# Attention and MoE on one core: the kv and z products a slot later, the numerator two slots behind the projection, and stage-one transfers in written order

## The chip, the cores and the metric

The program runs on one core of one Trainium2 chip. The metric is device time of one execution in microseconds (us), measured over the whole program. A profiled execution also gives a span, from the first to the last instruction of the program, and a trace of every engine: PE (matmul), PEld (its weight loads), DVE (VectorE), ACT (ScalarE), POOL (GpSimd), SP (the engine whose queue issues nearly all transfers here), and the DMA engines.

## What is computed

A linear attention over 8 batches of 8 heads, 576 positions, head size 64, whose output is the input of a two-layer MoE block of 4608 tokens. Cut to what matters:

```python
def phi(x):
    proj = np.einsum('bhsd,df->bhsf', x, w_phi)               # 64 -> 128 features
    proj = proj - np.max(np.abs(proj), axis=-1, keepdims=True)
    return np.concatenate([np.exp(proj), np.exp(-proj)], axis=-1)
q_p, k_p = phi(q), phi(k)
kv  = np.einsum('bhsf,bhsd->bhfd', k_p, v)
z   = np.sum(k_p, axis=2)
num = np.einsum('bhsf,bhfd->bhsd', q_p, kv)
den = np.einsum('bhsf,bhf->bhs', q_p, z)[..., None] + 1e-06
x   = (num / den)                                              # to [4608, 512]
h   = x @ w_in                                                 # [4608, 2048]
g   = np.maximum(h, 0.0) + alpha * np.minimum(h, 0.0)
out = g @ w_out                                                # [4608, 512]
```

## The kernel before

The work has two stages. **Stage one** runs over 32 pairs of heads (`i`, four pairs for each batch of the attention). Beside the pairs it runs the first 5 of 16 slices of the MoE's middle dimension for the first seven blocks of 512 tokens (`ffn1_units(c)`, c from 0 to 6), and it decodes weights. **Stage two** runs the other slices for all tokens, after a short piece that finishes the first five slices for the last two blocks.

The order of stage one is written by hand. Each piece of work has a time in *slots*, where pair i has its projections from slot i on. `AT` gives the times of a pair's pieces relative to i. All pieces of all pairs are sorted by time (`todo`) and recorded in that order. For PE this order is kept as it is (`manual_schedule`, line 449). The other engines, the SP queue among them, get an order from a scheduler that plans with estimated durations; a few instructions (`keep_in_program_order`) stand in the written place on their engine too. Each engine and the SP queue then work strictly in their order: one that waits holds up all that stands behind it.

The pieces of pair i, with their lines:

- `load` (192, 194): the transfers of raw keys and queries (`raw`, two buffers) and of `v` (three buffers).
- `project`, five times (207, 215, 216): PE multiplies into `pj` (two PSUM buffers), DVE takes the largest absolute value `m` and subtracts it, giving `t`. The first chunks hold keys, the last two queries, the third both.
- `k_exp` (232, 227): ACT makes `xk` (one buffer) and `k`. `k_sum` (240 to 242): the sums y and z, on POOL for i under 7, on DVE after that.
- `k_acc` (250) and `k_z` (260): PE multiplies into `kv`. `kv_out` (266) copies it to `ks`; `kv_turn` (271, 273) transposes it, giving `sf`.
- `q_exp` (287, 281, 289, 283): PE turns the queries, ACT makes `qf`.
- `num` (297, 304): the numerator, copied to `s`. `den` (311, 319, 321): the denominator; ACT copies it to `ds`, and a small transfer moves 9 values for each partition into `d9`.
- `invert` (327 to 332): DVE makes `r9` from `d9`; one transfer stores it to memory (`rec_d`), two read it back spread over partitions (`rr`).
- `finish` (338, 339): POOL multiplies `s` by `rr`, and a transfer stores the result (`x_d`).

A *filler* is one step of the MoE's first slices: three matmuls of 512 columns (367 to 369, or 373 to 375). `STEPS` places ten of them in each slot, so each block of tokens fills four slots (40 steps). A block begins with `fetch`, the transfer of four pairs' results (`xr`, 383), and `split` (389 to 392), in which DVE rounds `xr` to `xh` (line 94) and POOL takes the rest `xl` (line 97), four pieces each. `FL`, `FX` and `FO` place fetch, split and the first filler. I call the slot in which a block is fetched and split a *batch slot*.

`decode` (117 to 141) turns 64-bit weights into two 32-bit halves: a transfer (`raww`, two buffers), one ACT, four DVE and one POOL instruction, then one ACT and one POOL instruction (`w`, or `ow`). 20 blocks of it feed the first five slices, 20 more are stored back to memory (`w_d`, 141) for stage two.

## Time and profile before

| what | value |
|---|---|
| time, median of three runs | 1311.33 us (1309.7 to 1312.77) |
| time of the profiled execution | 1311.5 us |
| its span | 1309.7 us |
| PE busy | 1206.5 us (92%) |
| DVE, ACT, POOL busy | 658.2, 505.6, 345.1 us |
| mean granted TensorE clock, of full speed | 0.966 |

The profiled execution lies 0.2 us from the median, and 1.8 us of its time lie outside the span. Stage one runs to about 693 us of the span. The granted clock is 1.00 nearly throughout stage two, and lower in parts of stage one.

### The profile page before, as it was taken

Reading aid. Unit: us, or ns where it says so; the run is one execution under the profiler, and the core shown is the slowest. Engines: PE = TensorE matmul, PEld = TensorE weight load, DVE = VectorE, ACT = ScalarE, POOL = GpSimd, SP = SyncE. Lnnn points to the kernel's source line nnn. Section 1 sums busy time; section 2 is a strip of 40 time slices with the busy share of each in tenths; the row PEclk is TensorE's granted clock in tenths of the full one; section 3 lists DMA queues with packets and bytes.
Section 4 is the critical chain, followed back from the end, with each engine's and each line's share of the span. In section 5 each row is a group of like instructions: output and inputs, shape, how many; then the busy total and the mean of one; then the engine's idle time right before and its main releaser. Section 6 shows DMA issues by size and latency. Waiting matters only on the chain.

```text
span 1309.7 us, 16685 instructions
## 1 busy us (share of the span) xinstructions
PE 1206.5 (92%) x6272; PEld 919.4 (70%) x6272; DVE 658.2 (50%) x1112; ACT 505.6 (39%) x1014; POOL 345.1 (26%) x374
## 2 busy tenths in 40 slices
PE   5767799999989999997987999999999999999998
PEld 3434566677767667665755778888888888888886
DVE  4663566657666666667824357323333332323232
ACT  2543363555545455463633344222222222222221
POOL 4563422313132321324513246111111111111110
PEclk7789899999989999998998999999999999999999
DMA  4332334334343533525345032202022020202010
GB/s 154 95 113 85 106 100 154 124 122 126 124 137 109 165 104 102 164 92 174 103 143 191 33 131 63 97 1 97 25 72 71 26 97 1 97 1 97 1 66 32
DMA packets 67808, 124.20 MB, mean 95 GB/s; under 512 B 14224, under 2 KB 19472, under 8 KB 67088
## 3 DMA queue, kind: packets, MB, share of 16 engines
q1 hardware_dynamic: 67008, 117.90, 27.7%
q0 software_dynamic: 720, 5.24, 1.1%
q8 instruction: 49, 0.80, 0.3%
q14 instruction: 31, 0.25, 0.1%
HBM read 89.27 MB, written 33.70 MB: 94 GB/s over the span
## 4 chain that ended last, share of the span: by engine, by line
PE 71%; DMA 10%; DVE 7%; POOL 5%; issue 3%; ACT 2%; SPq 1%; DVEq 0%; POOLq 0%; ACTq 0%
PE h L367 9%; PE h L369 9%; PE h L368 9%; PE po L373 7%; PE po L374 7%; PE po L375 7%; PE pj L207 7%; PE kv L250 3%; DMA rr<-rec_d 3%; PE n L297 3%; PE d L311 2%; DMA xr<-x_d 2%; DMA rec_d<-r 2%; PE o L373 2%; PE o L374 2%
## 5 line engine op out<-in xcount | busy, mean ns | idle before, releaser
L207 PE MATMUL pj<-w_sb,raw 128*128 128x256 f32 x576 | 169.2, 418 | 44.1 <-DVE t L216 21.7
L150 ACT ACTIVATE r<-h 128x512 f32<-128x512 f32 x144 | 86.0, 598 | 283.6 <-PE h L369 283.1
L156 POOL TENSOR_SCALAR r<-r,al 128x512 f32<-128x512 f32 x99 | 73.1, 738 | 433.8 <-ACT r L150 429.0
L157 DVE SCALAR_TENSOR_TENSOR g<-h,r 128x512 f32<-128x512 f32 x99 | 68.2, 689 | 235.7 <-POOL r L156 235.7
L207 PEld LDWEIGHTS pj<-w_sb,raw 128*128 128x128 f32 x576 | 113.3, 206 | 86.6 <-issue 56.7
L215 DVE TENSOR_REDUCE m<-pj 128x4 f32<-128x512 f32 (+1 forms) x160 | 101.1, 635 | 111.3 <-PE pj L207 107.8
L373 PE MATMUL po<-gh,w 128*128 128x512 f32 x396 | 155.6, 393 | 0.0
L374 PE MATMUL po<-gh,w 128*128 128x512 f32 x396 | 155.2, 392 | 0.0
L93 ACT CAST gh<-g 128x512 fp32r<-128x512 f32 x144 | 89.3, 621 | 167.8 <-DVE g L157 134.6
L375 PE MATMUL po<-gl,w 128*128 128x512 f32 x396 | 153.6, 392 | 0.0
L97 DVE TENSOR_TENSOR gl<-g,gh 128x512 fp32r<-128x512 f32 x144 | 102.6, 713 | 72.6 <-ACT gh L93 72.6
L216 DVE TENSOR_TENSOR t<-pj,m 128x512 f32<-128x512 f32 (+1 forms) x160 | 101.2, 633 | 2.8
L367 PE MATMUL h<-x2hl,w 128*128 128x512 f32 x220 | 87.0, 396 | 11.9 <-ACT x2hl L93 11.9
L338 POOL TENSOR_TENSOR s<-s,rr 128x576 f32<-128x576 f32 x31 | 46.4, 1497 | 194.0 <-DMA rr<-rec_d 163.9
L373 PE MATMUL o<-gh,w 128*128 128x512 f32 x180 | 86.0, 478 | 2.1 <-ACT gh L93 1.1
L367 PE MATMUL h<-xh,w 128*128 128x512 f32 x180 | 86.4, 480 | 1.2 <-ACT g L152 1.2
L369 PE MATMUL h<-x2hl,w 128*128 128x512 f32 x220 | 86.7, 394 | 0.0
L368 PE MATMUL h<-x2hl,w 128*128 128x512 f32 x220 | 86.6, 394 | 0.0
L375 PEld LDWEIGHTS po<-gl,w 128*128 128x128 f32 x396 | 74.4, 188 | 17.0
L374 PEld LDWEIGHTS po<-gh,w 128*128 128x128 f32 x396 | 74.4, 188 | 16.8
L373 PEld LDWEIGHTS po<-gh,w 128*128 128x128 f32 x396 | 74.3, 188 | 16.7
L250 PE MATMUL kv<-xk,v 128*64 128x256 f32 x512 | 68.9, 416 | 17.7 <-ACT xk L232 17.7
(82 smaller groups left out, 2228.7 us busy)
## 6 DMA issues: line engine op xcount, KB each, us to landing
raw<-kq_dram SPq DMA_DIRECT2D x32, 576.0 KB
xr<-x_d SPq DMA_DIRECT2D x17, 1024.0 KB
v<-v_dram SPq DMA_DIRECT2D x32, 320.0 KB
rr<-rec_d SPq DMA_DIRECT2D x64, 144.0 KB
x_d<-s SPq DMA_DIRECT2D x32, 288.0 KB
part_d<-os SPq DMA_DIRECT2D x36, 256.0 KB
pt<-part_d SPq DMA_DIRECT2D x9, 1024.0 KB
raww<-w_in_dram SPq DMA_DIRECT2D x32, 256.0 KB
```

What stands on the lines that cost most here:

```text
L93: return act.copy(dst, src)
L97: return eng.tensor_tensor(dst, src, f(hi), op=ALU.subtract)
L207: pe.matmul(ps[:, j].rearrange("p h f -> p (h f)"), lhsT=c["raw"][:, tp * P : (tp + 1) * P], rhs=w_sb, start=True, stop=True,)
L215: dve.tensor_reduce(m, ps, axis=AX.X, op=ALU.max, apply_absolute_value=True)
L216: dve.tensor_tensor(c["t", ch][:, :, j0 : j0 + w].rearrange("p h j f -> p j h f"), ps, m.unsqueeze(3).broadcast_to([P, w, 2, FD]), op=ALU. ...
L250: pe.matmul(c["kv"][h * D : (h + 1) * D, 0], lhsT=c["v"][:, tp, h, :], rhs=c["x", ch][:, :, h, j, :], start=tp == 0, stop=False,)
L367: pe.matmul(ps, lhsT=wt[0][:, ws], rhs=xh, start=n == 0, stop=False)
L368: pe.matmul(ps, lhsT=wt[1][:, ws], rhs=xh, start=False, stop=False)
L369: pe.matmul(ps, lhsT=wt[0][:, ws], rhs=xl, start=False, stop=n == NK - 1)
L373: pe.matmul(ps, lhsT=wt[2][:, ws], rhs=gh, start=first, stop=False)
L374: pe.matmul(ps, lhsT=wt[3][:, ws], rhs=gh, start=False, stop=False)
L375: pe.matmul(ps, lhsT=wt[2][:, ws], rhs=gl, start=False, stop=last)
```

## The change

A pair's pieces are spread over more slots. The products `kv` and `kz` go from 0.48 and 0.50 to 1.17 and 1.18, one slot behind the pair's projections; numerator and denominator go from 1.49 and 1.505 to 2.16 and 2.155, two slots behind. The turned queries (`q`), the turned kv (`kr`), `invert` (`dv`) and `finish` (`x`) follow. `load` moves from 1.3 to 0.95 slots ahead. A block of tokens begins three steps later (`FO`), and its fetch and split stand after the slot's start instead of before it (`FL`, `FX`). `decode` is split: the transfer of the raw weights is an entry of its own, half a slot ahead (`WL`). The SP queue joins PE: in stage one its transfers are issued in written order.

```diff
-WS = 1.4
-W2A = 7.0
+WS = 1.6
+WL = 0.5
+W2A = 8.5
...
-    ld=-1.3,
-    p=(0.0, 0.12, 0.24, 0.80, 0.90),
-    ke=(0.14, 0.25),
-    ks=0.29,
-    q=(1.27, 1.33, 1.39),
-    ka=0.48,
-    n=1.49,
-    kz=0.50,
-    d=1.505,
-    kt=0.51,
-    kr=1.17,
-    dv=1.95,
-    x=2.35,
+    ld=-0.95,
+    p=(0.0, 0.08, 0.50, 0.82, 0.92),
+    ke=(0.20, 0.51),
+    ks=0.515,
+    n=2.16,
+    d=2.155,
+    ka=1.17,
+    kz=1.18,
+    kt=1.185,
+    q=(1.55, 1.62, 1.66),
+    kr=1.75,
+    dv=2.60,
+    x=3.00,
 )
-STEPS = (0.05, 0.08, 0.16, 0.20, 0.30, 0.36, 0.42, 0.45, 0.85, 0.95)
+STEPS = (0.03, 0.06, 0.11, 0.13, 0.52, 0.57, 0.64, 0.70, 0.86, 0.96)
 EARLY = 7
-FO = 4
+FO = 7
 F0 = 3.0
-FL = 0.4
-FX = 0.2
+FL = -0.2
+FX = -0.4
...
+    wraw = {}
+
+    def decode_load(ff, z, o, n):
...
-        ld_ = nc.sync.dma_start(raw.rearrange("p a b -> p (a b)"), (w_in, w_out)[z][ff][:, cs].bitcast(U32))
-        if NF1 <= ff < NF1 + NA:
-            tc.keep_in_program_order(ld_)
+        nc.sync.dma_start(raw.rearrange("p a b -> p (a b)"), (w_in, w_out)[z][ff][:, cs].bitcast(U32))
+        wraw[ff, z, o] = raw
+
+    def decode(ff, z, o, n):
+        tag = f"w{ff}_{z}_{o}"
+        if (ff, z, o) not in wraw:
+            decode_load(ff, z, o, n)
+        raw = wraw.pop((ff, z, o))
+        cs = slice(o, o + n)
...
-                todo.append(((ff + z / 2) * WS, lambda ff=ff, z=z, o=o: decode(ff, z, o, WN)))
+                t = (ff + z / 2 + o / 1024) * WS
+                todo.append((t - WL, lambda ff=ff, z=z, o=o: decode_load(ff, z, o, WN)))
+                todo.append((t, lambda ff=ff, z=z, o=o: decode(ff, z, o, WN)))
...
+        todo.append((t - WL, lambda blk=blk: decode_load(*blk, WN)))
         todo.append((t, lambda blk=blk: decode(*blk, WN)))
...
-    with tc.manual_schedule(engines={mybir.EngineType.PE}):
+    with tc.manual_schedule(engines={mybir.EngineType.PE, mybir.EngineType.SP}):
```

Three places show what moves. The first is PE in the early slots, where no fillers run yet. In the names the digit behind the first letters is the pair: kv3 is the kv product of pair 3, d2 the denominator of pair 2. Before, from the turned queries of pair 2 to its denominator:

```order
L287 MATMUL qt2_1_602<-ident_67,t2_3_514 128x128 x4
L281 MATMUL qt2_t_611<-ident_67,t2_2_434 128x128 x2
L250 MATMUL kv3_616<-xk3_571,v3_365 64x256 x8
L250 MATMUL kv3_616<-k4_1_121,v3_365 64x256 x2
L297 MATMUL n2_0_628<-qf2_589,sf2_579 64x288 x4
L297 MATMUL n2_1_634<-qf2_589,sf2_579 64x288 x4
L260 MATMUL kv3_616<-z3_598,ones_117 64x256 x2
L311 MATMUL d2_666<-qf2_589,sf2_579 32x288 x8
L207 MATMUL pj3_3_686<-w_sb_115,raw3_363 128x256 x2
```

Now, the same products of pairs 2 and 3, which stand behind two projections of pair 4:

```order
L216 MATMUL pj4_0_634<-w_sb_115,raw4_491 128x256 x2
L216 MATMUL pj4_1_654<-w_sb_115,raw4_491 128x256 x2
L320 MATMUL d2_660<-qf2_572,sf2_614 32x288 x8
L306 MATMUL n2_0_674<-qf2_572,sf2_614 64x288 x4
L306 MATMUL n2_1_680<-qf2_572,sf2_614 64x288 x4
L259 MATMUL kv3_686<-xk3_544,v3_346 64x256 x8
L259 MATMUL kv3_686<-k4_1_121,v3_346 64x256 x2
L269 MATMUL kv3_686<-z3_568,ones_117 64x256 x2
L216 MATMUL pj4_2_717<-w_sb_115,raw4_491 128x256
L296 MATMUL qt3_0_730<-ident_67,t3_3_616 128x128 x4
```

The kv product of pair 3 stood in the slot of that pair's own projections; it now stands in pair 4's, and d2 stands ahead of z3 instead of behind it.

The second place is the SP queue around the fetch of the first block of tokens (xr1_0). Before, from the denominator of pair 2:

```order
L321 DMA d9_2_677<-ds2_675 128x1x9
L192 DMA raw5_681<-kq_dram 128x1152
L329 DMA rec_d_58<-r9_2_698 128x9
L332 DMA rr2_702<-rec_d_58 64x576 x2
L339 DMA x_d_57<-s2_627 128x576
L194 DMA v7_1003<-v_dram 128x640
L321 DMA d9_3_824<-ds3_822 128x1x9
L192 DMA raw6_828<-kq_dram 128x1152
L329 DMA rec_d_58<-r9_3_869 128x9
L332 DMA rr3_873<-rec_d_58 64x576 x2
L339 DMA x_d_57<-s3_798 128x576
L383 DMA xr1_0_975<-x_d_57 128x4x512
```

Now, from the denominator of pair 3:

```order
L330 DMA d9_3_820<-ds3_818 128x1x9
L124 DMA raww3_1_256_869<-w_out_dram 128x512
L338 DMA rec_d_58<-r9_3_886 128x9
L341 DMA rr3_890<-rec_d_58 64x576 x2
L124 DMA raww4_0_0_929<-w_in_dram 128x512
L348 DMA x_d_57<-s3_822 128x576
L201 DMA raw7_956<-kq_dram 128x1152
L203 DMA v7_958<-v_dram 128x640
L330 DMA d9_4_977<-ds4_975 128x1x9
L392 DMA xr1_0_1010<-x_d_57 128x4x512
L124 DMA raww4_0_256_1012<-w_in_dram 128x512
L338 DMA rec_d_58<-r9_4_1055 128x9
```

The raw keys of a pair stood behind the denominator's transfer three pairs earlier and now stand behind the store of x_d four pairs earlier; raw weights stand between; the fetch has the next pair's denominator transfer ahead of it.

The third place is DVE around the split of the fourth block of tokens (xh1_3; m17_3 is the m of pair 17, chunk 3). Before:

```order
L215 TENSOR_REDUCE m17_3_3219<-pj17_3_3216 128x4
L216 TENSOR_TENSOR t17_3_3215<-pj17_3_3216,m17_3_3219 128x2x2x128
L94 CAST xh1_3_3222<-xr1_3_3209 128x512 x4
L215 TENSOR_REDUCE m17_4_3255<-pj17_4_3252 128x4
L215 TENSOR_REDUCE m18_0_3273<-pj18_0_3270 128x4
L216 TENSOR_TENSOR t17_3_3215<-pj17_4_3252,m17_4_3255 128x2x2x128
L327 TENSOR_SCALAR d9_16_3205<-d9_16_3205 128x9
L216 TENSOR_TENSOR t18_0_3269<-pj18_0_3270,m18_0_3273 128x2x2x128
```

Now:

```order
L137 TENSOR_SCALAR aw7_0_256_3310<-aw7_0_256_3310 128x256
L138 SCALAR_TENSOR_TENSOR aw7_0_256_3310<-raww7_0_256_3208,aw7_0_256_3310 128x256
L139 TENSOR_SCALAR ew7_0_256_3311<-aw7_0_256_3310 128x256
L140 SCALAR_TENSOR_TENSOR ew7_0_256_3311<-raww7_0_256_3208,ew7_0_256_3311 128x256
L95 CAST xh1_3_3259<-xr1_3_3257 128x512 x4
L224 TENSOR_REDUCE m18_2_3272<-pj18_2_3270 128x2
L249 TENSOR_TENSOR y18_3277<-xk18_3254 128x1024
L225 TENSOR_TENSOR t18_2_3269<-pj18_2_3270,m18_2_3272 128x256
L250 TENSOR_TENSOR z18_3278<-y18_3277 128x512
L251 TENSOR_TENSOR z18_3278<-z18_3278,k4_0_119 128x512
L336 TENSOR_SCALAR d9_16_3224<-d9_16_3224 128x9
L224 TENSOR_REDUCE m18_3_3348<-pj18_3_3345 128x4
```

The split stood ahead of the slot's first two projections' m; it now stands behind them and ahead of the third's, with the sums y and z between it and the fourth's; a block of decoding (aw7, ew7) stands ahead of it.

## Rows read from the trace of the kernel before

**Rows 1.** The page: busy us, share of the span and instructions of each engine.

```profile
PE 1206.5 (92%) x6272; PEld 919.4 (70%) x6272; DVE 658.2 (50%) x1112; ACT 505.6 (39%) x1014; POOL 345.1 (26%) x374
```

**Rows 2.** Stretches: length; busy PE, PEld, DVE, ACT, POOL; clock, DMA. Slots 0 to 6.

```profile
5.90:27.10 21.20, 13.47 (x42) 7.94 (x42) 11.16 (x26) 6.98 (x14) 10.61 (x11) 0.76 0.41 146
...
99.80:118.20 18.40, 12.42 (x88) 7.76 (x88) 6.11 (x13) 7.23 (x15) 6.26 (x4) 1.00 0.29 83
...
sum 154.60, PE 109.21 PEld 69.41 DVE 83.81 ACT 62.95 POOL 75.93; mean PE 15.60 PEld 9.92 DVE 11.97 ACT 8.99 POOL 10.85
```

**Rows 3.** The same for slots 7 to 31, three of the 25.

```profile
373.00:399.20 26.20, 21.13 (x120) 15.35 (x119) 15.55 (x22) 9.19 (x19) 7.47 (x6) 0.87 0.32 112
399.20:417.50 18.30, 18.30 (x120) 13.50 (x119) 13.79 (x24) 10.54 (x23) 5.22 (x5) 1.00 0.36 112
...
591.80:619.20 27.40, 18.46 (x119) 13.31 (x117) 20.16 (x37) 11.19 (x26) 12.46 (x12) 0.91 0.53 169
...
sum 498.80, PE 468.03 PEld 340.99 DVE 342.06 ACT 260.36 POOL 145.66; mean PE 18.72 PEld 13.64 DVE 13.68 ACT 10.41 POOL 5.83
```

**Rows 4.** Waits of PE in slots 0 to 6: total, times, longest.

```profile
PE kv L250 <- ACT xk L232: 16.2, 6, 3.4
PE kv L260 <- POOL z L242: 16.2, 7, 3.9
```

**Rows 5.** Waits of PE in slots 7 to 31.

```profile
PE pj L207 <- DVE t L216: 15.9, 5, 5.1
PE pj L207 <- issue: 9.2, 2, 9.0
```

**Rows 6.** The chain of waits, 107 to 126 us: start, length, what.

```profile
107.40 1.41 POOL s L338
108.81 2.32 POOL y L240
...
114.51 1.11 PE d L311 x16
...
120.28 2.07 DMA rec_d<-r
...
122.89 2.91 DMA rr<-rec_d
```

**Rows 7.** PE in order of time: two projections, then two fillers.

```profile
452.53 1.02 PE L207 MATMUL pj<-w_sb,raw 128*128 128x256 f32 x4
...
454.09 1.02 PE L207 MATMUL pj<-w_sb,raw 128*128 128x256 f32 x4
...
672.30 0.39 PE L373 MATMUL o<-gh,w 128*128 128x512 f32 x1
...
672.98 0.39 PE L373 MATMUL o<-gh,w 128*128 128x512 f32 x1
```

**Rows 8.** Chain of waits in a batch slot; POOL's pieces over the program (min/median/max ns).

```profile
368.04 6.94 DMA xr<-x_d
375.00 3.56 DVE xh L94 x4
...
L97 POOL TENSOR_TENSOR xl<-xr,xh x36: 1260/1416/1715, 137.1 to 723.7; 128x512 fp32r<-128x512 f32 x36
```

**Rows 9.** From the last denominator to stage two: chain of waits, then PE.

```profile
669.08 1.15 PE d L311 x16
...
670.73 5.71 DMA d<-ds
...
693.23 0.79 PE L367 MATMUL h<-x2hl,w 128*128 128x512 f32 x1 [11.93 <-ACT x2hl L93]
```

**Rows 10.** One decoding instruction: early slots, whole program; two weight issues on SP.

```profile
L131 DVE SCALAR_TENSOR_TENSOR ew<-raww,ew 128x256 f32<-128x256 uint32 x20 | 12.1, 614 | 0.3
...
L131 DVE SCALAR_TENSOR_TENSOR ew<-raww,ew x64: 404/419/1517, 13.3 to 809.1; 128x256 f32<-128x256 uint32 x64
...
609.27 8.41 SPq L121 DMA_DIRECT2D raww<-w_out_dram  x2
```

More of the change, by code (lines that the diff above doesn't have):

```diff
@@ L115, in weight_tile @@
         return [t[:, n, :] for n in range(4)], t
-    def decode(ff, z, o, n):
+    wraw = {}
+    def decode_load(ff, z, o, n):
         tag = f"w{ff}_{z}_{o}"
```

## The prediction

> **What bounds the kernel now.** PE is busy for 92% of the span [rows 1], so the first question is where it is not. I read the stretches slot by slot. A slot with ten fillers takes 18.30 us when PE never stops, at granted clock 1.00 (399.2 to 417.5 in [rows 3]). Ten fillers are 10 x 0.68 = 6.8 us (672.30 and 672.98 in [rows 7]), so one pair alone is 11.5 us of PE. Against these two numbers stage one loses time in three places.
>
> First, slots 0 to 6 take 154.6 us after a start of 5.9 [rows 2], though hardly a filler runs there: 22 us a slot where PE has 11.5 of work. The waits of PE there are two, 16.2 us each: kv for ACT's xk, kz for POOL's z [rows 4]. The chain of waits shows a closed loop [rows 6]: POOL's s ends at 108.81, then y and z on POOL, then kz, then d on PE, ending at 115.62 (6.8 us). Then d9, rec_d and rr bring the next s 10.4 us after that (126.0), and it takes 1.4. The loop is 18.6 us, and a slot without decoding takes 18.4 [rows 2].
>
> Second, slots 7 to 31 take 498.8 us where 25 x 18.30 = 457.5 would do. Of the excess of 41, 15.9 us are PE waiting for t, five times, and 9.0 one wait that the profile names no releaser for [rows 5]; both fall in the batch slots, where DVE does the split. With the lower clock that follows a long one (0.87 in the slot of 26.2 us, [rows 3]) the six of them lose some 33; the remaining 8 are kv and kz waits.
>
> Third, stage two waits for the last pair. From the end of the last d (670.2) to the first matmul of stage two (693.2) are 23.0 us, of which PE is idle 11.9 [rows 9].
>
> The sum is made on the profiled span, 1309.7; the program's time is 1.8 above it, and 0.2 above the median.
>
> **Part one: kv, z, numerator and denominator in later slots.** The work on PE is the same, matmul for matmul. What goes is the loop. d of pair i is now ahead of kz of pair i+1 on PE, and k_sum of pair i has until the next slot. So y and z are out of the chain of the early slots: POOL's s of pair i must come before k_sum of pair i+3, whose d stands two slots later still, so the old loop now spans three slots. What is late next is SP. Its queue is in written order, and there d9 of a pair stands behind x_d of the pair before it. One turn is: d to s, 10.4 us; s, 1.4; the issues of x_d, raw, v and a weight load, some 0.4 each with gaps between (0.4 is an issue of SP as the trace has them; estimate 1.2 in all). That is 13.0 us, near PE's 11.5 plus the waits of p0 and p1 for t.
>
> To that comes decoding. In slots 0 to 3 before, 20 blocks were decoded, in 93.9 us; four slots without would have taken 73.6, so a block cost 1.0 us. Now a slot has 2.5 blocks: 13.0 + 2.5 = 15.5 us. Slot 0 holds only projections (11 us: DVE was busy 11.2 in its stretch, [rows 2]), slot 1 no numerator (12, between 8.5 of PE work and 15.5). Slot 6 has three fillers (2.0) and waits for the first split (2.5, see below): 20. Start of slot 7: 5.9 + 11 + 12 + 4 x 15.5 + 20 = **110.9 instead of 160.5, a gain of 49.6**. Bounds: with 13.0 a slot and shorter first ones 95; with 18.4 a slot, 18.6 loop kept, 126. I take the middle, as the loop is gone by the order of PE itself.
>
> Slots 7 to 31 lose their kv and kz waits, 8 us, to nothing: kv comes a full slot behind k_exp.
>
> **Part two: fetch and split later, three fillers later.** In the new order the fetch stands on SP behind d9 of the next pair. Two projections and four fillers (2 x 0.88 + 4 x 0.68, [rows 7]) and d (1.1) are ahead of that: d ends at 5.6 us in the slot, d9 goes out at 6.2, xr at 6.9. It takes 6.9 [rows 8]: landed at 13.8. DVE's four xh take 3.6, POOL's first xl 1.4 more [rows 8]. PE reaches the new block's first filler at 14.1 (18.3 less kt, two projections and three fillers) and must have xh and xl: 1.2 us late. DVE ends xh at 17.4, then m, y, t of the third projection (some 2.2): the fifth projection, which needs that PSUM buffer, comes at 19.7 instead of 18.0, 1.7 late. Then z twice, d9, m and t (3.1): the next slot's p0 at 22.7, 1.4 late. Sum 4.3, and 0.7 for a lower clock: 5.0 for each of six batch slots, 30 us. So the stall moves from the slot's end to its last third but stays: **slots 7 to 31 take 457.5 + 30 = 487.5 instead of 498.8, a gain of 11.3**. Bounds: no stall (the fetch lands early), a gain of 41; the worst that the trace has of its kind, 7.9 us in the slot of 26.2, six times: a loss of 6. I take 5.0, near the mean of the five in [rows 5] with their clock.
>
> **Part three: the tail.** More work stands behind slot 31: in slot 32 ten fillers and all of a pair but its projections (6.8 + 7.3), in slot 33 four fillers and d (3.9); then the same 23.0 us chain to stage two. 14.1 + 3.9 + 23.0 = 41.0 instead of 33.9 (659.3 to 693.2): **a loss of 7.1**. Behind the last d, PE has n (1.9) and 13 fillers (8.8), before 16 fillers (10.9): the idle stretch stays some 12 us. Bounds +-3: SP has part_d stores between the chain's transfers in either order.
>
> **Part four: raw weights half a slot ahead, SP in written order.** The loads now wait for a raw buffer (two of them), in a place of the queue where rec_d, rr, x_d and raw stand behind. I cost this at nothing in slots 7 to 31: SP's turn of 13.0 us plus four more issues is 14.6, which leaves 3.7 us of waits in 18.3 free, and raw is asked for 0.95 slots ahead where it lands in about 5. In the early slots it is in the 1.0 us a block. Stage two has the same code: 0, +-3.
>
> **Sum.** 1309.7 - 49.6 - 11.3 + 7.1 = 1255.9 of span, with 1.8 outside: **1257.7 us, 4.1% faster**.
>
> **The rivals.**
> *DVE and POOL get in each other's way* once early slots are dense. One decoding instruction of DVE took 0.61 us in the early slots and 0.42 as median of the program [rows 10]; the projections' m and t read PSUM and kept their time. If every POOL instruction of a slot held DVE, a slot would be POOL's 10.0 us (k_sum 4.9, s 1.4, 2.5 x 1.46 of decoding) plus DVE's 9.8: 19.8 x 4 instead of 62: 1275. Against it: the row shows 0.2 us for an instruction, not an exclusion. The Trainium skill, GPSIMD Engine Reference, section Specifications, says that the two share SBUF interfaces and contend where DVE has two SBUF inputs or a two-port mode; L131 has two SBUF inputs, so this trace agrees as far as 0.61 against 0.42 goes. By that rule the decoding's 1.0 us could grow and nothing else.
>
> *SP's written order holds up the queue, slower than before.* In 609 to 618 two weight issues held SP for 8.4 us [rows 10]. If a weight load or its w_d store waited 8.4 us in each of the 20 slots with a block, and in series with the turn of 14.6, a slot would be 23.0: 20 x 4.7 = 94 us more, 1352, slower. It decides from 3.7 us of such waits in a slot, and makes the kernel slower than before from about 6.4. For it: 40 loads stand where the queue must not stop. Against it: half a slot (9 us) is the lead, and the waits for DVE and POOL in the turn run beside such a wait. The Trainium skill, DMA: Bandwidth & Descriptors, section Anatomy of one DMA, says that DMA engines do not wait for semaphores, the issuing sequencer does so before it dispatches. The 8.4 us on SP is that in this trace, and it is the rule that speaks against this change. *A half of it* (5 us in series in those slots) gives 20 x 1.3 = 26: 1284.
>
> *The batch slots stop stalling*, since three fillers' delay covers the fetch: 1257.7 - 30 = 1228. Against it the sum above, where the fetch is behind d9.
>
> **How the numbers follow.** 0.2% of this kernel, 2.6 us, is about what a measurement can tell from no change. Forecast (1242 to 1273, early slots between 13 and 18 us): 0.63. DVE and POOL (1275): 0.09. Half of SP's waits (1284): 0.12. No stall in the batch slots (1228): 0.09. SP in full, slower: 0.05. Early gain and SP loss that cancel, within 0.2%: 0.02. The range 1233 to 1287 leaves out the last two and most of the no-stall case, so under 0.2. Faster: 0.63 + 0.09 + 0.12 + 0.09 = 0.93; same 0.02; slower 0.05.
>
> **What would show it.** Slot 7's first projection near 111 us; no kv or kz waits of PE behind the first two slots; slots of 18.3 us between batch slots; in batch slots a wait of a filler for xl, then of pj for t, 4 to 5 us together; 41 us from the last pj to stage two. Wrong would be: early slots above 18 us; SP weight issues that wait over 4 us in most slots, with rr, x_d or raw late behind them; pj waiting for raw.

## The result, and the profile after

The changed kernel took 1317.2 us (median, 1314.2 to 1320.8) beside 1312.1 us of the kernel before on the same chip: ratio 1.0043, 95% interval 1.0025 to 1.0061. It is slower by 0.4%, where 4.1% faster was forecast. Each experiment below ran beside the kernel before, on a chip whose median for that kernel lay between 1310.5 and 1312.8 us; where the text subtracts the times of two kernels, up to some 2 us of it can be the chip. The profiled execution has a span of 1315.3 us, 5.6 more than before.

The page, answering [rows 1], shows almost nothing: PE is busy 5 us longer in a span 6 us longer.

```profile
PE 1211.1 (92%) x6272; PEld 914.1 (69%) x6272; DVE 660.7 (50%) x1112; ACT 503.3 (38%) x1014; POOL 347.5 (26%) x374
```

The stretches tell more (columns as in [rows 2]): slots 0 to 6, slots 7 to 31, one plain slot (20), one batch slot (22), and from slot 31's end to stage two.

```profile
5.90:124.50 118.60, 90.49 (x523) 59.00 (x524) 81.91 (x154) 56.20 (x126) 69.42 (x63) 0.90 0.38 127
124.50:656.70 532.20, 481.92 (x2948) 341.19 (x2949) 345.16 (x590) 262.07 (x560) 152.12 (x146) 0.97 0.38 120
401.00:420.40 19.40, 18.80 (x119) 13.36 (x118) 13.39 (x26) 11.65 (x25) 4.73 (x6) 1.00 0.37 112
440.70:466.00 25.30, 20.73 (x119) 14.03 (x118) 13.34 (x20) 8.45 (x17) 7.79 (x5) 0.93 0.40 133
656.70:699.80 43.10, 32.26 (x187) 21.73 (x186) 9.32 (x19) 14.82 (x30) 6.40 (x7) 0.90 0.46 155
```

Against [rows 2, 3, 9]: the early slots gained 36.0 us (154.6 to 118.6), slots 7 to 31 lost 33.4 (498.8 to 532.2), the tail lost 9.2 (33.9 to 43.1), stage two gained 1.0 (693.2 to the end, 616.5, now 699.8 to the end, 615.5). Sum: 5.6 lost. Over 18.30 us a slot, slots 7 to 31 lose 74.7: 43.2 in the six batch slots, where the forecast had 30, and 31.5 in the 19 plain ones, where it had nothing. The plain slots, 18.30 before wherever PE did not stop, are now 18.4 to 21 (slot 7 is 24.2); the six batch slots are 23.6 to 29.4.

The waits of PE in slots 7 to 31 (total, times, longest), where [rows 5] had pj for t and one long wait:

```profile
PE pj L216 <- issue: 18.7, 14, 3.0
PE kt L280 <- ACT qf L298: 10.9, 13, 2.3
PE pj L216 <- DVE t L225: 9.3, 6, 3.7
PE h L376 <- DVE xh L95: 8.5, 5, 4.2
```

The kv and kz waits of [rows 4] are gone, as forecast. New is kt, 23.9 us in the program: kt takes the PSUM buffer that q0 had, and so waits for the exps of q0 (qf) on ACT. The waits named "issue" are p0 of a slot; in each of them the t of the p3 before ended 0.1 us ahead of p0, on DVE. Six of them, 12.9 us in all, end the batch slots. Of the 31.5 us of the plain slots, 10.9 are PE's waits at kt, 4.2 at p0, 3.7 one wait for t in slot 7, and 12.3 are PE busy longer (the granted clock is 0.92 or 0.93 in slots 7, 11 and 19). ACT and DVE now let PE wait in slots where they did not before.

What holds ACT is seen in the plain slot 20 (SP, then ACT in order of time, then kt on PE):

```profile
407.71 0.33 SPq L348 DMA_DIRECT2D x_d<-s  x1
...
409.74 0.46 SPq L124 DMA_DIRECT2D raww<-w_out_dram  x1
```

```profile
410.76 2.01 ACT L241 ACTIVATE xk<-t 128x1024 f32<-128x1024 f32 x2 [0.43 <-PE kv L259]
413.77 0.45 ACT L136 ACTIVATE aw<-raww 128x256 f32<-128x256 f32 x1 [1.00 <-DMA raww<-w_out_dram]
414.12 0.56 ACT L275 COPY ks<-kv 128x512 f32<-128x512 f32 x1
414.59 0.72 ACT L236 ACTIVATE k<-t 64x256 f32<-64x256 f32 x2
415.21 2.02 ACT L298 ACTIVATE qf<-qt 128x512 f32<-128x512 f32 x4
```

```profile
416.32 0.66 PE L280 MATMUL kt<-ident,ks 128*128 128x128 f32 x4 [0.30 <-ACT qf L298]
```

There is one buffer for xk, and kv now reads it a slot later. So xk can begin only when kv is done (410.7), and xk, ks, k and the two exps of q0 all stand between kv and kt: 2.0 + 0.6 + 0.7 + 1.0 = 4.3 us on ACT, where PE needs 5.3 to reach kt (416.0). The block's step aw and the 1.0 us that ACT stands for its raw weight are more than what is left. That weight was asked for at 409.7, behind x_d, for which SP had stood until 407.7. In the kernel before xk came ahead of its kv in the same slot, and the next to want qf was n, behind kv.

The batch slot 22 (440.7 to 466.0), SP's issues, then DVE and PE, where [rows 8] has the transfer:

```profile
445.67 0.33 SPq L348 DMA_DIRECT2D x_d<-s  x1
...
448.10 0.59 SPq L330 DMA_DIRECT2D d<-ds  x1
448.79 0.53 SPq L392 DMA_DIRECT2D xr<-x_d  x1
...
456.25 3.59 DVE L95 CAST xh<-xr 128x512 fp32r<-128x512 f32 x4 [10.78 <-DMA xr<-x_d]
...
456.74 0.50 PE L376 MATMUL h<-xh,w 128*128 128x512 f32 x1 [1.73 <-DVE xh L95]
...
458.19 0.50 PE L378 MATMUL h<-xl,w 128*128 128x512 f32 x1 [0.73 <-POOL xl L98]
...
462.44 1.14 PE L216 MATMUL pj<-w_sb,raw 128*128 128x256 f32 x4 [0.39 <-DVE t L225]
...
466.03 1.10 PE L216 MATMUL pj<-w_sb,raw 128*128 128x256 f32 x4 [1.74 <-issue]
```

The four waits are those of the forecast (first filler for the split, the fifth projection for t, the next p0), but xr goes out 8.1 us into the slot instead of 6.9, and the casts begin 15.5 us into it instead of 13.8. The clock costs more than the 0.7 us of the forecast too: PE is busy 20.73 us at a mean granted clock of 0.93 (3.4 us of the slot, from 459.1 on, stand at the lower of its two levels, 1.2 GHz; PE had stopped twice shortly before), beside 18.30 in a slot without stops.

### The profile page after: what moved, and what is told of

Same layout as the page of the kernel before. It is cut to its first block, busy times and chain, and to the rows that moved or that the text cites. A ratio compares the mean times of both kernels' runs of the same rounds, so it can differ in the third digit from the quotient of the medians.

```text
span 1315.3 us, 16675 instructions
## 1 busy us (share of the span) xinstructions
PE 1211.1 (92%) x6272; PEld 914.1 (69%) x6272; DVE 660.7 (50%) x1112; ACT 503.3 (38%) x1014; POOL 347.5 (26%) x374
## 4 chain that ended last, share of the span: by engine, by line
PE 61%; DMA 14%; DVE 9%; issue 6%; ACT 5%; POOL 3%; SPq 2%; DVEq 0%; POOLq 0%; ACTq 0%
PE h L376 8%; PE h L378 8%; PE h L377 8%; PE po L382 7%; PE po L383 7%; PE po L384 7%; PE pj L216 5%; DMA xr<-x_d 4%; DMA rr<-rec_d 4%; DVE xh L95 2%; DMA rec_d<-r 2%; DMA raww<-w_out_dram 2%; PE n L306 2%; ACT xk L241 2%; PE d L320 1%
## 5 line engine op out<-in xcount | busy, mean ns | idle before, releaser
L216 PE MATMUL pj<-w_sb,raw 128*128 128x256 f32 x576 | 171.3, 422 | 43.6 <-issue 25.3
L216 PEld LDWEIGHTS pj<-w_sb,raw 128*128 128x128 f32 x576 | 109.9, 206 | 87.4 <-issue 60.1
L376 PE MATMUL h<-xh,w 128*128 128x512 f32 x180 | 91.6, 509 | 13.4 <-DVE xh L95 12.2
L141 POOL TENSOR_TENSOR aw<-ew,aw 128x256 f32<-128x256 f32 x64 | 48.5, 760 | 147.1 <-DVE ew L140 138.5
```

What stands on the lines that cost most here:

```text
L216: pe.matmul(ps[:, j].rearrange("p h f -> p (h f)"), lhsT=c["raw"][:, tp * P : (tp + 1) * P], rhs=w_sb, start=True, stop=True,)
L376: pe.matmul(ps, lhsT=wt[0][:, ws], rhs=xh, start=n == 0, stop=False)
```

## The experiments

The tables and sums below come from each kernel's own trace in the same way: slot 7's start is its first projection, a slot's loss is its length over 18.31 us. They are those of one execution each; that of the lag alone (1306.9 us) was 5.6 us below the kernel's median, that of SP freed (1292.5) 3.4 below. Ratios are to the kernel before, run beside it.

### Lag or transfers?

The first four ask which half of the change loses. The lag alone, on the kernel before (shown: three of its lines; AT, STEPS, FO, FL and FX are all as in the change):

```diff
-    ka=0.48,
+    ka=1.17,
...
-FL = 0.4
+FL = -0.2
```

> The lags, the fillers' steps and the places of fetch and split as in the changed kernel (AT, STEPS, FO, FL, FX); transfers and raw weights as before (SP ordered by the planner, weights requested with their block). Theory 1, written order of transfers: in the changed kernel a raw weight stands on SP behind x_d, which waits for POOL's s, so it lands late, ACT stands at its aw with xk, ks and qf behind it, and kt waits for qf. Then here PE's waits of kt for qf fall from 23.9 us to under 6, plain slots come to 18.3 to 18.6, slot 7 starts some 10 us earlier, and the time is 1285 to 1297. Theory 2, the lag itself: kt takes the PSUM buffer of q0 and waits for its exps whatever SP does; kt's waits stay above 18 us and the time is 1312 to 1320.

Measured: 1312.5 us, ratio 1.0008 (0.9984 to 1.0033). Slot 7 starts at 123.5, slots 7 to 31 take 523.8. PE's waits of kt for qf are 48.8 us, twice as long as with the written order. Theory 1, that the written order makes them, falls; the time is that of theory 2.

The transfers alone, the changed kernel with the AT, STEPS, FO, FL and FX of before:

```diff
-    ka=1.17,
+    ka=0.48,
...
-FL = -0.2
+FL = 0.4
```

> The other half: SP in written order, raw weights half a slot ahead and the new spacing of the blocks, with the lags, steps, fetch and split of the kernel before. Theory 1 (written order is the loss): slower than before, since a raw weight behind x_d stops ACT here too, 1320 to 1345. Theory 2 (the lag is the loss): within 4 us of before, 1308 to 1316.

Measured: 1310.7 us, ratio 0.9993 (0.9976 to 1.0011). Slots 0 to 6 cost 10 us more than before (slot 7 at 170.4), slots 7 to 31 cost 10 less (488.3). With the old lags written order does no harm over the program, although ACT stands 70.5 us at aw for raw weights there (42.1 in the kernel before).

SP freed, in the changed kernel:

```diff
-    with tc.manual_schedule(engines={mybir.EngineType.PE, mybir.EngineType.SP}):
+    with tc.manual_schedule(engines={mybir.EngineType.PE}):
```

> The changed kernel with one edit: SP is no longer in written order, the planner places its transfers; loads stay separate from their decoding. Theory 1: as for the lag alone, 1285 to 1297, kt's waits for qf under 6 us in all. Theory 2: 1312 to 1320, kt's waits above 18 us.

Measured: 1296.0 us, ratio 0.9874 (0.9831 to 0.9917). It is as fast as theory 1 wanted, but not by its reason: the waits of kt for qf are 45.8 us. What the planner did with a free SP was to draw all blocks that are left of stage one, and the eight of stage two's next weights, into slots 7 to 13. ACT's decoding step aw in two stretches (length; busy, count), then all engines in slots 15 to 17 and in slot 11:

```profile
125.00:305.00 180.00, 11.48 (x26) 0.94 0.50 155
306.00:617.00 311.00, 0.00 (x0) 0.98 0.33 105
```

```profile
306.40:362.00 55.60, 55.49 (x355) 40.50 (x356) 33.32 (x56) 29.92 (x62) 7.93 (x8) 1.00 0.31 97
219.60:244.10 24.50, 20.18 (x120) 14.58 (x119) 18.60 (x37) 15.06 (x34) 12.64 (x14) 0.93 0.48 146
```

Where nothing is decoded, three slots take 55.6 us and PE does not stop. In slots 7 to 13 a plain slot takes 20.0 to 24.5. That made decoding the suspect. The run does not settle what written order costs, since the blocks moved with it.

The ring of PSUM buffers, tried by moving kt behind both later projections:

```diff
-    kr=1.75,
+    kr=1.93,
```

> The changed kernel with one number changed: kt at 1.93 of a slot instead of 1.75, behind both later projections, so that it reaches its PSUM buffer some 3.3 us later in a slot. Theory 1: ACT is late by what SP brings late; kt's waits fall to under 8 us, but p0 and the next d get part of the lateness, 1300 to 1310. Theory 2: the ring of three PSUM buffers ties kt to q0 and that is the whole of the plain slots' loss: kt's waits under 3 us, plain slots 18.3 to 18.6, 1285 to 1298.

Measured: 1312.3 us, ratio 1.0012 (0.9986 to 1.0039), 0.3% less than the changed kernel's ratio, with intervals that overlap, and outside both ranges. The waits of kt fall to 3.5 us, and those of p0 ("issue") rise from 25.3 to 33.4: the lateness moves on. The same edit on the kernel with SP free:

> The kernel with SP free (1296) and kt at 1.93 of a slot instead of 1.75. There PE's waits of kt for qf are 45.8 us, in the early slots and in slots 7 to 14 where 28 blocks are decoded. If PE's order (kt ahead of the last projections) turns ACT's lateness into PE's: 1270 to 1285. If the lateness only moves on to p0 and d: 1290 to 1300.

Measured: 1289.4 us, ratio 0.9842 (0.9807 to 0.9876): 6.6 us off the 1296.0, a little below the range in which the lateness only moves on. Here too the greater part of the lateness moves on, to p0.

### Decoding

The 20 blocks of slots 8 to 30 left out, first in the changed kernel, then in the kernel before (the load of the five weights is replaced by loads of the same size from `kq`; the output is not the reference's):

```diff
-    blocks = [(ff, z, o) for ff in range(NF1, NF1 + NA) for z in range(2) for o in range(0, 512, WN)]
+    blocks = []
```

> The changed kernel without the 20 weight blocks that are decoded between slots 8 and 31 (left out; stage two's first five weights are then loaded from another input of the same size, so its output is not the reference's). Theory 3, decoding against the new lags: a block puts two steps into ACT's in-order queue ahead of qf, kt stands right behind qf on PE, and DVE's steps of the block stand ahead of m and t. Then plain slots come to 18.3 to 18.7, PE's waits of kt for qf fall under 14 us (those of the early slots), slots 7 to 31 take 500 to 512 instead of 532, and the time is 1284 to 1298. Theory 1, SP's written order holds the queue without weights too: plain slots stay at 19 to 20 and the time at 1308 to 1318.

> The kernel before with the same 20 blocks left out in the same way. Theory 3: the old lags give ACT and DVE room for a block, so that little is to be gained: 1302 to 1310. If decoding costs both kernels alike (some 1.0 us a block): 1288 to 1296.

Measured: 1291.7 us, ratio 0.9858 (0.9816 to 0.9900), and 1307.2 us, ratio 0.9974 (0.9954 to 0.9994). Over the program the same 20 blocks cost the changed kernel some 25 us and the kernel before 3. The 3 hides a shift. Without its blocks the kernel before takes 484.5 us in slots 7 to 31, 14.2 less than with them, and 10.9 more in slots 0 to 6, into which the planner drew ten steps aw of the next weights (aw on ACT, 30 of them where 20 stood; columns as above):

```profile
5.90:171.40 165.50, 13.11 (x30) 0.87 0.37 118
```

In slots 10 to 28, where neither of the two kernels without blocks decodes anything, the blocks cost 22.8 us with the new lags and 7.5 with the old. Theory 3 stands in kind: decoding is dearer beside the new lags, by three times and not by eight. The stretches of the changed kernel without blocks: slots 7 to 31 and a plain slot.

```profile
123.50:628.60 505.10, 471.40 (x2948) 337.88 (x2949) 313.63 (x510) 249.93 (x520) 118.89 (x106) 0.99 0.33 106
391.30:409.70 18.40, 18.40 (x119) 13.60 (x119) 12.17 (x22) 10.72 (x22) 2.85 (x4) 1.00 0.28 90
```

From slot 10 on the plain slots are nearly the forecast's (18.4 to 18.8, one 20.0). The batch slots lose 4.6 each on average, where 5.0 was forecast. Of the 505.1, slots 7 to 9 hold 14.4 over 18.31 each: the next eight blocks, of the weights that stage two decodes, were drawn there by the planner.

Is it the raw weight that comes late, or the work? Requested a whole slot ahead:

```diff
-        todo.append((t - WL, lambda blk=blk: decode_load(*blk, WN)))
+        todo.append((t - 1.0, lambda blk=blk: decode_load(*blk, WN)))
```

> The changed kernel with the raw weights of those 20 blocks requested a whole slot ahead instead of half a slot. If ACT's standing for a raw weight that lands late (49 us of ACT's waits in slots 9 to 31) is what makes qf, kt and p0 late: plain slots 18.4 to 19.0 and 1298 to 1308. If it is the work of a block on ACT, DVE and POOL itself: within 4 us of the changed kernel, 1312 to 1321.

Measured: 1319.6 us, ratio 1.0077 (1.0053 to 1.0102): no gain. By its expectation that speaks for the work. But ACT still stood 86.8 us at aw for raw weights (76.5 in the changed kernel). A block of slot 24, SP's issue and ACT's step:

```profile
493.49 0.46 SPq L124 DMA_DIRECT2D raww<-w_out_dram  x1
```

```profile
498.85 0.43 ACT L136 ACTIVATE aw<-raww 128x256 f32<-128x256 f32 x1 [2.14 <-DMA raww<-w_out_dram]
```

This block's decoding is written for slot 25, and its request for slot 24. ACT was ready for the weight 3.2 us after it went out (496.7), in slot 24, and stood 2.1 us, until 5.4 after: ACT is not in written order, and the planner had moved aw forward with the load. So this run didn't test what it was made for. The next holds aw where it is written:

```diff
-        act.activation(f(a), hi.bitcast(F32), AF.Copy, scale=2.0**-112)
+        aw = act.activation(f(a), hi.bitcast(F32), AF.Copy, scale=2.0**-112)
+        if ff < NF1 + NA:
+            tc.keep_in_program_order(aw)
```

> The changed kernel with one edit: ACT's first step of every block of stage one (aw) is held in written order on ACT, behind what is written ahead of it. Theory 3a: the planner puts aw where it takes the raw weight as landed, earlier than it lands on the chip, whatever lead SP gives it; ACT then stands (76 us at aw in all) with qf behind it, and kt stands on PE. Then here ACT's waits at aw fall under 25 us, PE's waits of kt for qf under 12 us, and the time is 1290 to 1305. Theory 3b: it is the work of a block on ACT, DVE and POOL, wherever it stands: 1310 to 1320.

Measured: 1303.3 us, ratio 0.9941 (0.9926 to 0.9955), 14 us off. The waits of ACT at aw and of PE at kt, whole program, in this kernel:

```profile
ACT aw L136 <- DMA raww<-w_in_dram: 13.8, 13, 5.9
...
ACT aw L136 <- DMA raww<-w_out_dram: 1.3, 3, 0.6
```

```profile
PE kt L282 <- ACT qf L300: 12.3, 9, 2.2
```

ACT's 76.5 us at aw are 15.1 now, kt's 23.9 are 12.3, and the loss of the plain slots falls from 31.5 us to 17.4, which is the whole gain. Theory 3a is right for these 14 us. Next the place of the block as well, one in each slot, right behind the numerator's copies:

```diff
-        t = W2A + (W2Z - W2A) * n / len(blocks)
-        todo.append((t - WL, lambda blk=blk: decode_load(*blk, WN)))
+        t = 9.17 + n
+        todo.append((t - 0.9, lambda blk=blk: decode_load(*blk, WN)))
```

> As the pinned kernel, and the 20 blocks between slots 9 and 29 stand one in each slot at the same place, behind the copies of the numerator, where DVE, ACT and POOL had been idle; their raw weights are requested 0.9 slots ahead. Theory 3a or 3b alike, if the place decides: plain slots 18.3 to 18.7 as without the blocks, 1288 to 1296. If a block costs its 1.0 us anywhere: 1305 to 1315.

Measured: 1312.1 us, ratio 1.0009 (0.9993 to 1.0025). The number lies in the range of "a block costs its 1.0 us anywhere", but not for that reason, since two things happened. A plain slot (17) and a batch slot (22):

```profile
330.30:348.70 18.40, 18.40 (x119) 13.61 (x119) 11.74 (x21) 8.74 (x19) 3.33 (x3) 1.00 0.43 127
431.70:460.50 28.80, 21.60 (x120) 15.40 (x119) 14.67 (x24) 8.86 (x19) 10.08 (x8) 0.82 0.50 145
```

The plain slots have a block each and lose next to nothing (18.4 to 18.7 from slot 11 to slot 27). Five of the six batch slots lose 8.6 to 10.5, the last 7.0. SP in that batch slot shows why: the store of the block (w_d) waits for POOL's ow, and xr stands behind it.

```profile
438.26 0.58 SPq L332 DMA_DIRECT2D d<-ds  x1
445.45 0.37 SPq L152 DMA_DIRECT2D w_d<-ow  x1
445.91 0.42 SPq L394 DMA_DIRECT2D xr<-x_d  x1
```

### When the fetch goes out

xr 14.2 us into a batch slot is some 9 to 10 us lost. Can it be early? Fetch directly behind its x_d, and the inversion ahead of y and z:

```diff
-    dv=2.60,
+    dv=2.505,
...
-FL = -0.2
+FL = -0.02
```

> The changed kernel with the fetch of a batch directly behind its x_d on SP (instead of behind d9 of the next pair) and the inversion 0.095 slots earlier, ahead of y and z on DVE. If the batch slots' excess (43 us in six, 28 without blocks) is the late landing of xr: xr lands 3 us earlier in its slot, no wait of a filler for xh, 3 to 5 us less in each of the six, 1290 to 1302. If it is the 3.6 us of casts on DVE ahead of m and t, wherever they stand: 1309 to 1318.

Measured: 1274.6 us, ratio 0.9730 (0.9708 to 0.9752). Two numbers take 43 us off the changed kernel, more than expected. Each alone:

> The changed kernel with the inversion alone earlier (2.505 instead of 2.60: r9 ahead of most of y and z on DVE, rec_d ahead on SP). Theory 4, SP stands at rec_d and x_d for DVE and POOL in every slot, and raw weights, d9 and xr stand behind: rec_d, s, x_d and xr each come some 3 us earlier, and most of the 43 us is here: 1278 to 1292. Theory 5, the place of the fetch behind d9 is the loss: 1308 to 1318.

> The changed kernel with the fetch alone moved, directly behind x_d on SP. Theory 4: x_d itself is late and xr has to wait until it has landed, so xr gains under 1 us: 1308 to 1318. Theory 5: 1278 to 1292.

Measured: the inversion alone 1303.6 us, ratio 0.9930 (0.9908 to 0.9951); the fetch alone 1295.7 us, ratio 0.9887 (0.9853 to 0.9921). Both theories gave one of the two the whole; it is neither: 14 and 22 us alone, 43 together. SP in the batch slot 22 of the three (slot's start 436.9, 427.1 and 412.5), inversion alone, fetch alone, both:

```profile
439.04 0.33 SPq L348 DMA_DIRECT2D x_d<-s  x1
...
443.21 0.59 SPq L330 DMA_DIRECT2D d<-ds  x1
443.90 0.43 SPq L392 DMA_DIRECT2D xr<-x_d  x1
```

```profile
431.69 0.33 SPq L348 DMA_DIRECT2D x_d<-s  x1
...
433.85 0.37 SPq L392 DMA_DIRECT2D xr<-x_d  x1
```

```profile
415.10 0.33 SPq L348 DMA_DIRECT2D x_d<-s  x1
...
417.28 0.37 SPq L392 DMA_DIRECT2D xr<-x_d  x1
```

With the inversion alone x_d goes out 2.2 us into the slot, but xr stands behind d9, which waits for PE's d of this slot: 7.0. With the fetch alone xr no longer waits for d9, but x_d is as late as ever (4.6) and must land first: 6.8. With both, 4.8. Each edit takes away one of two waits of which the later counts.

That is the batch slots' part. Of the 38.0 us that the two together take off slots 7 to 31, 26.0 lie in the batch slots and 12.0 in the plain ones, although ACT at aw and PE at kt wait as long as in the changed kernel (76.5 and 23.9 us over the program):

```profile
ACT aw L136 <- DMA raww<-w_in_dram: 50.7, 22, 5.1
...
ACT aw L136 <- DMA raww<-w_out_dram: 26.1, 17, 4.9
```

```profile
PE kt L280 <- ACT qf L298: 25.7, 15, 4.0
```

What did change is the way from d to s. From the end of a pair's d on PE to the start of its s on POOL, as a mean of pairs 7 to 27, the kernel before takes 12.6 us, the changed one 18.7, the inversion alone 15.1, both edits 13.9.

All together, with aw pinned, one block a slot and kt late:

> All of it together: aw pinned, one block a slot behind the numerator's copies, fetch and inversion early, and kt at 1.93. If the three losses are separate: 25 us of decoding, 15 to 25 of the batch slots and 5 of kt off 1317: 1262 to 1275. If they share their cause: 1280 to 1290.

> aw pinned on ACT, with fetch and inversion early as in the kernel at 1274.6. If decoding and the late x_d are separate losses, the 14 us that pinning gave come off again: 1258 to 1266. If an earlier x_d had already brought the raw weights in time: 1270 to 1277.

Measured: all together 1270.0 us, ratio 0.9696 (0.9673 to 0.9720), in the range of three separate losses. But the number came by luck, for the other run shows that they are not separate: aw pinned, fetch and inversion early, no spacing and kt as it was: 1302.3 us, ratio 0.9927 (0.9899 to 0.9954), 28 us slower than without the pin. The expectation saw no loss there. A pinned aw is later, so ow is, and SP stands at w_d, ahead of rec_d: SP's wait of w_d for POOL's ow is 28.2 us in the changed kernel, 21.0 with fetch and inversion early, 151.4 with the pin beside them, 137.9 in the combined kernel. So this wait is not the whole of the 28 us: it is nearly as long in the combined kernel, which is 32 us faster. Spacing and kt, in which the two differ, were not tried one by one.

The casts of the split behind m and t of the third projection, in the combined kernel:

```diff
-FX = -0.4
+FX = -0.503
```

> The combined kernel (1270) with the split's casts one place later on DVE, behind m and t of the third projection. There the six batch slots still lose 3 to 5 us each, 2 of it PE at p4 for t. If m of the third projection behind 3.6 us of casts is the cause: 1256 to 1264. If the casts only meet PE's first filler instead: 1268 to 1276.

Measured: 1278.5 us, ratio 0.9736 (0.9709 to 0.9763), slower than without and outside both ranges: the wait of p4 goes, and the next p0 waits 3.1 us instead.

The last two take SP's wait at w_d away, by moving the store of a block behind rr (the first's edit, cut):

```diff
-            nc.sync.dma_start(w_d[ff - NF1, :, 2 * z : 2 * z + 2, cs], f(t))
+            wout[ff, z, o] = t
...
+        todo.append((t + 0.338, lambda blk=blk: decode_store(*blk, WN)))
```

> The combined kernel (1270) with the store of each decoded block moved on SP from behind d9 to behind rr. If SP standing at w_d is what makes rec_d, x_d and xr late there: x_d goes out under 2.5 us into a batch slot and xr under 4.5, the six lose under 2 us each instead of 3.8, slots 7 to 31 take 475 to 483 instead of 490.6, and the time is 1255 to 1263. If rec_d waits for r9 on DVE anyway: 1266 to 1273.

> The same with aw of the next eight blocks (of the weights that stage two decodes beside its first part) held in written order on ACT too, so that they stay out of slots 29 to 31. If they cost their 6 us there and nothing in stage two: 1249 to 1257. If stage two pays for them: no gain over the kernel beside it, or a loss of some us.

Measured: 1257.6 us, ratio 0.9592 (0.9573 to 0.9612), and with aw of the next eight blocks pinned too 1262.0 us, ratio 0.9620 (0.9601 to 0.9640). The first is 54 us faster than the kernel before and the fastest here; x_d and xr (on average), the stretch and the time came as expected, but a batch slot still loses 2.6 us and not under 2. In the second slots 7 to 31 take 472.6, but stage two takes 10 us more: it pays for the blocks. The stretches of the first: slots 7 to 31, a plain slot, a batch slot.

```profile
121.90:600.60 478.70, 462.15 (x2945) 335.87 (x2946) 347.18 (x593) 261.81 (x559) 162.34 (x147) 1.00 0.41 135
311.90:330.20 18.30, 18.30 (x119) 13.49 (x118) 11.41 (x21) 8.77 (x20) 3.81 (x3) 1.00 0.43 132
406.30:427.10 20.80, 18.74 (x119) 13.23 (x118) 15.23 (x23) 8.95 (x20) 9.99 (x7) 1.00 0.41 147
```

The runs in one table: where xr goes out in the six batch slots (mean, us into the slot), what such a slot loses, slot 7's start and the length of slots 7 to 31.

| kernel | us | xr | batch slot loses | slot 7 at | slots 7 to 31 |
|---|---|---|---|---|---|
| changed | 1317.2 | 8.7 | 7.2 | 124.5 | 532.2 |
| aw pinned, one block a slot | 1312.1 | 13.3 | 9.2 | 125.0 | 524.3 |
| aw pinned | 1303.3 | 9.3 | 6.6 | 124.4 | 514.6 |
| inversion early | 1303.6 | 8.0 | 6.0 | 126.3 | 521.6 |
| aw pinned, fetch and inversion early | 1302.3 | 8.2 | 6.4 | 124.8 | 518.9 |
| fetch ahead | 1295.7 | 6.1 | 5.1 | 119.2 | 516.2 |
| no blocks | 1291.7 | 7.0 | 4.6 | 123.5 | 505.1 |
| fetch and inversion early | 1274.6 | 3.7 | 2.9 | 119.9 | 494.2 |
| all together | 1270.0 | 6.8 | 3.8 | 120.2 | 490.6 |
| and the store later | 1257.6 | 4.4 | 2.6 | 121.9 | 478.7 |
| and the next aw pinned | 1262.0 | 3.9 | 2.2 | 119.8 | 472.6 |

(For the inversion alone the profiled execution, 1306.7 us of span, was above that kernel's median.)

## Why the prediction was wrong

**The sum.** The forecast's span was 1255.9, the profiled one 1315.3: 59.4 missed. Of these 44.7 lie in slots 7 to 31 (487.5 forecast, 532.2 came), 13.6 in the early slots, 2.1 in the tail, and stage two gave 1.0 back.

**The step that failed: part four, "I cost this at nothing in slots 7 to 31".** The plain slots were to stay at 18.30; they lose 31.5 us. Two terms were wrong.

The first is SP's turn, 14.6 us of 18.3, and in it "d to s, 10.4 us". That was read from an early slot of the kernel before and carried over. For pairs 7 to 27 of the changed kernel it is 18.7 on average (14.4 to 24.9), so the 3.7 us called free were not there. r9 ends 11.2 us after d9 goes out, 5.1 in the kernel before: the inversion stands in written order on DVE, behind y and z, which need xk. SP stands meanwhile, in slots 7 to 31:

```profile
SPq L338 <- DVE r L337: 190.6, 20, 16.7
```

The second is a term put at nothing without a reason: what a raw weight holds up on ACT. ACT takes its steps in order, the order is the planner's, and the planner moved aw up with the request, to where the weight had not landed; in slot 20 ks, k and qf stand behind it, and by the ring of three PSUM buffers kt, with 1.0 us to spare. In the old order the same standing cost little: with the transfers alone it is 70.5 us, and slots 7 to 31 take 488.3.

What each is worth the runs bound, but do not separate. Of the 44.7 us, leaving out the blocks takes 27.1, and without the 14.4 of the next eight slots 7 to 31 would take 490.7 beside a forecast of 487.5. Holding aw back takes 14.1 off the plain slots. Inversion and fetch early take 38.0 off slots 7 to 31 with every block in its place and ACT standing as long as ever. So ACT's standing is not the loss by itself. Why it costs less once s, x_d and the fetch are early, no run shows. That a block's place and not its work is the price in a plain slot is shown by the kernel at 1257.6, where 18.3 us hold a block and a full slot.

**The batch slots: mechanism right, the fetch's time and the clock mis-sized.** The forecast said d9, then xr 6.9 us into the slot, and 5.0 us lost: a filler for xl, p4 for t, the next p0. The same waits came, with xh for the first filler, and with xr at 7.0 (no blocks) the loss was 4.6. But in the changed kernel xr goes out at 8.7 on average, and 7.2 are lost. Of the 13.2 us above the forecast in the six, 5 are waits; 8 are PE busy longer, 20.3 us a slot where 18.3 is a full one, at a granted clock under 1.00 in four of them. No row gave the 0.7 us that the forecast set for the clock. The forecast took d9 to be what holds the fetch; x_d is late too, since s waits for rr, rr for rec_d, and rec_d for r9. The rival "batch slots stop stalling" was right in kind: with xr at some 4 us the fillers no longer wait for the split; 2.6 us a slot are still lost, at p4 and the next p0.

**The early slots: right in kind, 13.6 too much.** No kv or kz wait of PE is left, and slot 7 starts near 120 in every kernel with the new lags, SP free or not, kt late or not (119.2 to 126.3). So the written order is not it. 15.5 a slot was forecast; slots 2 to 5 take 15.9 to 19.5. In slots 1 to 5 kt waits 13.0 us for qf, and in slots 2 to 4 the next p0 waits 6.7 for a t that stands behind decoding steps, some of which POOL's work stretches (last section). With kt late its early waits are 2.1 to 2.7 us, and slot 7 still starts at 120.2 and 121.9: the lateness moves on to p0. The rival of DVE and POOL, at 9 in 100, names a part of this; no run took POOL's k_sum away, so its share stays open.

**The tail: right.** 41.0 forecast, 43.1 came; the idle stretch ahead of stage two is 7.4 us instead of some 12, and a wait of 3.5 for a filler's gh stands earlier. Stage two: 0, +-3 forecast, 1.0 came.

**The rival on the other side.** "SP's written order holds up the queue" had the right sign. That its mechanism, SP's waits in series with its turn, decided the time is not shown: the lag alone, with SP free, gave 1312.5, and written order with the old lags 1310.7. It is not refuted either: the changed kernel with SP free gave 1296.0, 21 us less, though its blocks had moved too, and SP's stand at rec_d is such a wait. Written order does hurt where something that waits stands ahead of something that PE needs (d9 ahead of xr, w_d ahead of rec_d), and it is what made those places movable by a number: the fastest kernel is in written order. Nearest to what came was the rival to which the forecast gave 2 in 100, a gain and a loss that cancel: 36.0 us gained in the early slots, 42.6 lost behind them. That these two are of one size has no cause that the runs show.

**The range.** Its upper end, 1287, was made from SP's and POOL's prices. It took the turn of 14.6 us as a fact, and a term for ACT was missing altogether, though the two facts that make it, one buffer for xk and kv a slot later, stand in the code and the order of the changed kernel.

## What to carry to other kernels

When a change moves pieces to other slots, take each pair of neighbours on the bounding engine, add up what the engine between them has to do there, and set it against the time the bounding engine takes from one to the other: a margin of 1 us is gone as soon as anything else stands in that queue, even if no wait shows before. A latency read from the kernel before (d to s, 10.4 us) holds only as long as no step of its chain gets another place in an engine's order. When a transfer is late, look for all that it waits for: moving it past one wait gave 22 us, taking away the other 14, both 43. And a request that is written earlier did nothing here as long as the planner could move its first reader along with it; holding the reader back gave 14 us there, and cost 28 in the kernel with fetch and inversion early.

## What was not expected of the hardware

A small step on DVE stood still beside a step of POOL. In the early slots of the changed kernel the addition on d, 128 x 9 numbers, took 2.19 us while POOL did y, and it takes 0.17 otherwise (DVE, POOL, DVE):

```profile
59.83 2.19 DVE L336 TENSOR_SCALAR d<-d 128x9 f32<-128x9 f32 x1
```

```profile
59.62 2.36 POOL L249 TENSOR_TENSOR y<-xk 128x1024 f32<-128x1024 f32 x1 [3.27 <-ACT xk L241]
```

```profile
415.99 0.17 DVE L336 TENSOR_SCALAR d<-d 128x9 f32<-128x9 f32 x1
```

It ended when POOL's ended. So did all six additions on d of the changed kernel that began while a step of POOL had 0.3 us or more to go: each ended 0.03 us behind it. The decoding steps at L137 and L139 (one input in SBUF, beside a constant) ended 0.15 behind such a step of POOL, those at L138 and L140 (two inputs in SBUF) 0.28, with one exception in 28 (up to 700 us); the step at L138 took 0.41 us at the least and 1.45 at the most in slots 1 to 5. Not every step did so: the reciprocal on the same 128 x 9 numbers took 0.21 us beside y (at 42.12), and m and t, which read PSUM, kept their 0.69. So for these steps the forecast's "0.2 us for an instruction, not an exclusion", taken from a mean, was wrong: a single one waits for what is left of POOL's. The Trainium skill, GPSIMD Engine Reference, section Specifications, names two cases of this contention, two SBUF inputs of DVE or a two-port mode. The steps at L138 and L140 are the first case. The addition has one SBUF input, so by that rule it could only be the second; no run here shows in which mode it ran.
